# Fewer plain experts in the first token group, and three group change-overs laid out over two periods

## The chip, the cores and the metric

The kernel runs on one core of a Trainium2 chip. The metric is the device time of one execution in microseconds (us), as a median of several runs. The core's engines are TensorE (PE; its weight loads are listed apart as PEld), VectorE (DVE), ScalarE (ACT), GpSimd (POOL) and SyncE (SP), which here only issues DMAs. Each engine works off its own list of instructions in order.

## The reference, cut to what matters

A banded attention is followed by a first layer with an ELU between two matrix products, and by eight experts without routing: each token's row goes through every expert, and the results are added with weights P.

```python
x = attention(q, k, v)                      # 2304 tokens, 512 wide
h = x @ w_in                                # 512 -> 2048
x = elu(h) @ w_out                          # 2048 -> 512
P = exp(x @ w_gate - max)                   # 2304 x 8, then 8 rounds of
...                                         # row and column normalising
out = 0
for e in range(8):
    out += P[:, e:e + 1] * (maximum(x @ w1[e], 0) @ w2[e])   # 512 -> 1024 -> 512
```

## The kernel before, in words

All products are made at nearly full float32 precision: each operand is split into a high part (what the matmul keeps of it) and a low part (the rest), and three matmuls are added: high by high, high by low and low by high.

**The first layer** is cut into four hidden quarters ("layer pairs", `u` from 0 to 3). The last ends where the first expert matmul starts, at 554.8 us; it has 20 steps, each one hidden block of 128 for one block of up to 512 tokens. `step_in` makes the hidden values, `elu` turns them over on ACT and DVE, and `step_out` multiplies them out two steps later.

**The experts** take the 2304 tokens in three groups of 768. The first group (tokens 0 to 767, in blocks of 512 and 256) is computed **plainly** for all eight experts: `e_in` (lines 740 to 742) multiplies x by w1, `relu` splits the result, `e_out` (lines 758 to 760) multiplies by w2, and `e_done` (line 778) adds the weighted result to the accumulator `acc` on DVE. The steps are walked in units; from the second expert on a unit is half an expert (four hidden blocks of 128 for both token blocks, eight steps). I call that a **half**.

Groups 1 and 2 are computed **by a Strassen scheme**: the quarters of x, w1 and w2 are combined into seven forms each, so that seven products take the place of eight. A **period** `(g, e, pp)` is half an expert for one group: seven steps `j`, in each of which `l1` (line 914) makes two of the 14 products with the x forms `xf`, and `l2` (line 988) one of the seven products with the w2 forms, eight steps later (`LAG`). In `l1` PE adds up several products in one PSUM bank (`la`), and ACT copies the intermediate sums out (`keep`, line 927, tiles `a`, `u`, `v`) before PE may go on in that bank. DVE adds (`c`, lines 922 and 944; `s`, line 931), ACT and DVE split into high and low (`h`), POOL makes the low parts of the sums (line 896). DVE adds `l2`'s results into `acc2` (lines 1007 and 1009).

**The weight forms** are made once, while the first group runs, and do both jobs: a plain unit uses them in SBUF (the pure quarters, in one of eight slots `f0` to `f7`), and all seven are stored to DRAM (`wdi`, `wdo`) for the periods. There are 64 of them, `h = (expert * 4 + p) * 2 + m`. One form is five tasks (`p_tasks`): two pairs of sums on POOL (`p_sums`, line 645), two high parts on ACT (`p_high`, line 670), two low parts on DVE (`p_low`, line 675), two stores (`p_store`, lines 680 and 681) and the loads for the form after next but one (`p_load`, lines 631 and 636). The order of the work is written out by hand: at the end of each step the main loop runs as many tasks as a clock allows (`goal = 5 * (4 + clock / 3)`; a half is 12 clock units, so four forms a half). All DMAs go through SP's one queue.

**A change of group** needs new x forms. `x_load` fetches x from DRAM (`x2d`), `x_sums` and `x_t4` make four sums on DVE (line 833, 768 wide), and `x_form` makes each of the seven forms by a copy on ACT (line 828) and a subtraction on POOL (line 829). `x_steps` puts all of it in the last period of the old group: loads at step 0, the first form and three sums at step 2, the rest at steps 4 to 6. The first set of x forms is made in the last plain unit by the same functions. `oa` is the group's accumulator `acc2`; it has one buffer, so the first use by a new group waits for the stores of the old one's output (line 1012).

Of the kernel before, what the change touches and what calls it, by code (L numbers as in the profile page):

```python
# [8 lines left out]
F32 = mybir.dt.float32  # L9
# [9 lines left out]
def kernel(  # L19
# [14 lines left out]
    nc = tc.nc  # L34
# [578 lines left out]
    ]  # L613
    NHU = E * NP * 2
    rws, sws, forms = {}, {}, {}
# [4 lines left out]

    def p_load(h):
        if h >= NHU:
            return
        e, p, m = p_at(h)
# [38 lines left out]
    def p_high(h, part):  # L663
        if part == 0:
            b = h % 8
# [11 lines left out]
    def p_store(h):  # L677
# [3 lines left out]
        nc.sync.dma_start(out=to[:, 3:7], in_=r(forms[h][:, 4:8]))  # L681

    def p_tasks(h):
        def begin():
            p_sums(h, 0)

        def sums():
            p_sums(h, 1)  # L690
            if h:
                p_high(h - 1, 1)

        def lows():
            if h:
                p_low(h - 1, 1)

        def highs():
            p_high(h, 0)
            if h:  # L700
                p_store(h - 1)

        def last():
            p_low(h, 0)
            p_load(h + 3)

        def end():
            p_high(h, 1)
            p_low(h, 1)
            p_store(h)  # L710

        return [begin, sums, lows, highs, last] + ([end] if h == NHU - 1 else [])

# [9 lines left out]
    eunits = [(0, (0, 1)), (0, (2, 3)), (0, (4, 5, 6, 7))]  # L723
    eunits += [(e, tuple(range(4 * h, 4 * h + 4))) for e in range(1, E) for h in range(2)]

# [40 lines left out]
    def e_done(u, j, jj, pa):  # L766

        e, ch = eunits[u]
        a = acc[j][:, jj * DM:(jj + 1) * DM]
        tt = j * TB // P + jj  # L770
        if u == 0:
            nc.scalar.activation(a, pa, AF.Copy)  # L772
        elif e == 0:
            nc.vector.tensor_tensor(out=a, in0=pa, in1=a, op=ALU.add)
        else:
            if e == 1 and ch[0] == 0:
                nc.vector.tensor_scalar(a, a, Pr[:, tt, 0:1], None, op0=ALU.mult)
# [5 lines left out]
    x2d = {  # L783
        j: tc.dram_tile([P, NCC, n], F32, name=f"x2d{j}") for j, (t0, n) in enumerate(blocks)
        if t0 + n > 2 * TH
    }

    def x2_store(j):
        if j in x2d:
            nc.sync.dma_start(out=x2d[j], in_=acc[j].rearrange("p (c t) -> p c t", c=NCC))  # L790

# [42 lines left out]

    def x_sums():
        t1 = xs["pool"].tile([P, 2, TH], F32, tag="t1", name="xt1")
        t2 = xs["pool"].tile([P, 2, TH], F32, tag="t2", name="xt2")
        xs["t1"], xs["t2"] = t1, t2
        x_sum(t1, xs[0, 1], xs[0, 0])
        x_sum(t2, xs[1, 1], t1)  # L840
        x_sum(xs[0, 1], xs[1, 1], xs[0, 1])

    def x_t4():
        x_sum(xs[1, 0], xs[1, 0], xs["t2"])
        x_form(6, xs[1, 0])


    x_steps = {
        2: [lambda: x_form(0, xs[0, 0]), x_sums],
        4: [lambda: x_form(1, xs[1, 0]), lambda: x_form(4, xs["t2"])],  # L850
        5: [lambda: x_form(5, xs[0, 1]), lambda: x_form(3, xs["t1"])],
        6: [lambda: x_form(2, xs[1, 1]), x_t4],
    }

# [116 lines left out]
    def l2(k, x):  # L971
        g, e, pp = periods[k]
        pi = out_order[x]
        if x == 0:
            banks.reverse()
            ot["A"] = P2["ps2"].tile([P, 1024], F32, tag=banks[0], bufs=1, name=banks[0])
            if e == 0 and pp == 0:
                oa[g] = P2["ap"].tile([P, 6, DM], F32, tag="acc2", name="acc2")
# [39 lines left out]
    with tc.manual_schedule():  # L1018
# [127 lines left out]
        queue = []  # L1146
        extra = []
        for s, st in enumerate(steps):
            u, j, i = st
# [14 lines left out]
            if u == NU - 1:  # L1164
                if su == 2:
# [4 lines left out]
                    open_pool("A1", "right")  # L1170
                    for h in range(3):
                        p_load(h)
                    ptasks += p_tasks(0) + p_tasks(1) + p_tasks(2)[:3]
                elif su > 8 and ptasks:
                    ptasks.pop(0)()
            if extra:
# [5 lines left out]
        ]  # L1182
        ptasks += [f for h in range(2, NHU) for f in p_tasks(h)][3:]

        clock = 0
        ntask = 13
        done2 = False
        xq = []
        for s, st in enumerate(esteps):
# [24 lines left out]
            goal = 5.0 * (4.0 + clock / 3.0)  # L1214
            if s >= 2:
                lim = 5 * (NHU if done2 else 4) + 3
                while ptasks and ntask < min(goal, lim):
                    ptasks.pop(0)()
                    ntask += 1
            if u == len(eunits) - 1:  # L1220
                if (j, x) == (0, 1):
# [8 lines left out]
                    xq += [f for fs in x_steps.values() for f in fs]  # L1230
                for _ in range(2):
                    if xq:
                        xq.pop(0)()
# [12 lines left out]
        for s in range(NPD * 7 + LAG):  # L1246
# [8 lines left out]
            while after and k >= NPD:  # L1255
                after.pop(0)()
            if s == 1:
                for n in range(NW2):
                    w2_load(n)
            if s >= LAG:  # L1260
                l2(*divmod(s - LAG, 7))
                w2_load(s - LAG + NW2)
            if k + 1 < NPD and periods[k + 1][0] != periods[k][0]:
                if j == 0:
                    x_load(periods[k + 1][0])
                for f in x_steps.get(j, []):
                    f()
                if j == 6:
                    close(xs["cm"])
        close(ps2_cm)  # L1270
# [37 lines left out]
```

## Time and profile before

| what | us |
|---|---|
| three runs: median (lowest to highest) | 2081.74 (2080.84 to 2083.01) |
| the profiled execution: its own time | 2082.14 |
| its span, first to last instruction | 2080.1 |
| PE busy / DVE / ACT / POOL | 2042.9 / 1387.5 / 797.7 / 691.8 |
| the plain experts, first e_in to first l1 | 554.8 to 1109.7 |
| the 32 Strassen periods, first l1 to the end | 1109.7 to 2080.1 |

The profiled execution is 0.4 us above the median, and 2.0 us of its time lie outside its span. PE is busy nearly all the time, so a count of PE's busy time says little of where time could be saved; what counts is how long PE takes for a stage of known size, and where it is held up. The stretches are therefore compared by time for the same number of matmuls.

### The profile page before, as it was taken

How to read it: one execution, taken by the hardware profiler on the slowest of the kernel's cores; microseconds unless marked ns; L12 is line 12 of the kernel's file. 1: busy time of each engine (PE TensorE's matmuls, PEld its weight loads, DVE VectorE, ACT ScalarE, POOL GpSimd, SP SyncE). 2: the span in 40 equal slices, each digit the busy share in tenths (PEclk: the TensorE clock that was granted, in tenths of full speed). 3: DMA queues.
4: the chain of work that ended last, by engine and by line, in shares of the span. 5: the costliest groups of instructions: out<-in, count | busy, mean ns of one | idle time of the engine just before them, and what ended most of it. 6: DMA issues, size and time to landing. Idle time of an engine off the chain costs nothing.

```text
span 2080.1 us, 35944 instructions
## 1 busy us (share of the span) xinstructions
PE 2042.9 (98%) x13336; PEld 1866.0 (90%) x13336; DVE 1387.5 (67%) x2687; ACT 797.7 (38%) x1680; POOL 691.8 (33%) x698
## 2 busy tenths in 40 slices
PE   8999999999999999999999999999998999999998
PEld 6788888888878888888888999999998999999998
DVE  7944876754586555555555777777777777777776
ACT  5676333334442333333333333333334333333332
POOL 5533221220053434343333333233335323332332
PEclk9999999999999999999999999999999999999999
DMA  7631111110296878787777878787886887877874
GB/s 167 133 87 25 51 53 40 51 31 21 112 349 247 302 271 300 269 294 273 290 273 263 252 248 248 252 250 246 252 269 216 273 246 251 250 247 250 252 247 132
DMA packets 265469, 430.76 MB, mean 207 GB/s; under 512 B 75536, under 2 KB 139088, under 8 KB 260816
## 3 DMA queue, kind: packets, MB, share of 16 engines
q1 hardware_dynamic: 265216, 428.44, 63.4%
q8 instruction: 106, 1.74, 0.3%
q14 instruction: 67, 0.55, 0.1%
q10 hardware_dynamic: 80, 0.03, 0.0%
HBM read 302.53 MB, written 125.83 MB: 206 GB/s over the span
## 4 chain that ended last, share of the span: by engine, by line
PE 84%; DVE 6%; issue 6%; DMA 1%; POOL 1%; ACT 1%; SPq 0%; DVEq 0%; POOLq 0%; ACTq 0%
PE la L914 13%; PE ob L988 11%; PE oa L988 11%; PE lb L914 9%; PE ac L760 4%; PE ac L759 4%; PE ac L758 4%; PE p L740 4%; PE p L741 4%; PE p L742 4%; PE p L189 3%; PE p L191 2%; PE p L190 2%; PE ac L491 2%; PE ac L490 2%
## 5 line engine op out<-in xcount | busy, mean ns | idle before, releaser
L896 POOL TENSOR_TENSOR h<-s,h 128x384 fp32r<-128x384 f32 x256 | 314.2, 1246 | 620.7 <-ACT h L887 564.9
L914 PE MATMUL la<-xf,w1f 128*128 128x384 f32 x1536 | 307.7, 338 | 9.4 <-ACT u L927 5.1
L914 PEld LDWEIGHTS la<-xf,w1f 128*128 128x128 f32 x1536 | 264.8, 190 | 11.4 <-ACT u L927 6.0
L645 POOL TENSOR_TENSOR sw<-rw 128x256 f32<-128x256 f32 x128 | 123.7, 967 | 407.1 <-issue 203.9
L988 PE MATMUL oa<-w2f,h 128*128 128x256 f32 x2016 | 258.0, 282 | 1.1 <-DVE acc L1009 1.1
L988 PE MATMUL ob<-w2f,h 128*128 128x256 f32 x2016 | 258.7, 282 | 0.0
L988 PEld LDWEIGHTS oa<-w2f,h 128*128 128x128 f32 x2016 | 253.7, 190 | 1.4 <-DVE acc L1009 1.4
L988 PEld LDWEIGHTS ob<-w2f,h 128*128 128x128 f32 x2016 | 254.6, 190 | 0.0
L892 DVE SCALAR_TENSOR_TENSOR h<-c,h 128x384 fp32r<-128x384 f32 x192 | 176.2, 918 | 102.6 <-ACT h L887 102.0
L914 PE MATMUL lb<-xf,w1f 128*128 128x384 f32 x1152 | 232.8, 336 | 0.1
L232 DVE SCALAR_TENSOR_TENSOR hl<-p,hh 128x256 fp32r<-128x256 f32 (+1 forms) x128 | 71.1, 556 | 201.3 <-ACT hh L231 201.2
L914 PEld LDWEIGHTS lb<-xf,w1f 128*128 128x128 f32 x1152 | 201.1, 189 | 0.5 <-DVE c L944 0.4
L231 ACT ACTIVATE hh<-p 128x256 fp32r<-128x256 f32 (+1 forms) x128 | 62.8, 490 | 336.1 <-PE p L742 331.2
L887 ACT ACTIVATE h<-s 128x384 fp32r<-128x384 f32 x256 | 130.2, 523 | 121.4 <-DVE s L931 49.9
L740 PE MATMUL p<-xh,f 128*128 128x256 f32 (+1 forms) x512 | 174.0, 340 | 0.0
L741 PE MATMUL p<-xl,f 128*128 128x256 f32 (+1 forms) x512 | 173.0, 338 | 0.0
L742 PE MATMUL p<-xh,f 128*128 128x256 f32 (+1 forms) x512 | 172.5, 337 | 0.0
L1009 DVE SCALAR_TENSOR_TENSOR acc<-oa,Pr,acc 128x256 f32<-128x256 f32 x330 | 138.7, 474 | 37.8 <-PE oa L988 37.8
L887 ACT ACTIVATE h<-c 128x384 fp32r<-128x384 f32 x192 | 100.5, 523 | 148.0 <-DVE c L922 104.9
L1009 DVE SCALAR_TENSOR_TENSOR acc<-ob,Pr,acc 128x256 f32<-128x256 f32 x318 | 133.6, 474 | 34.6 <-PE ob L988 34.6
L758 PE MATMUL ac<-f,hh 128*128 128x512 f32 x384 | 151.9, 396 | 2.2 <-ACT acc L772 2.2
L760 PE MATMUL ac<-f,hl 128*128 128x512 f32 x384 | 151.7, 395 | 0.3 <-DVE hl L232 0.3
(147 smaller groups left out, 3954.0 us busy)
## 6 DMA issues: line engine op xcount, KB each, us to landing
w1f<-wdi SPq DMA_DIRECT2D x448, 256.0 KB, 3.8
w2f<-wdo SPq DMA_DIRECT2D x224, 512.0 KB, 4.0
rw<-in_moe_w_dram SPq DMA_DIRECT2D x256, 128.0 KB, 2.8
wdi<-f SPq DMA_DIRECT2D x32, 1024.0 KB, 6.0
wdo<-f SPq DMA_DIRECT2D x32, 1024.0 KB, 5.5
wdi<-f SPq DMA_DIRECT2D x32, 768.0 KB, 4.1
wdo<-f SPq DMA_DIRECT2D x32, 768.0 KB, 4.3
raw<-in_moe_w_in_dram SPq DMA_DIRECT2D x16, 512.0 KB, 3.9
```

What stands on the lines that cost most here:

```text
L645: nc.gpsimd.tensor_tensor(out=sw[:, o], in0=a, in1=b, op=op)
L740: nc.tensor.matmul(p1[:, :n], w[:, s, 0, cs], xh, start=(c == 0), stop=False)
L741: nc.tensor.matmul(p1[:, :n], w[:, s, 0, cs], xl, start=False, stop=False)
L742: nc.tensor.matmul(p1[:, :n], w[:, s, 1, cs], xh, start=False, stop=(c == NCC - 1))
L758: nc.tensor.matmul(o, gh[:, tcs], wh, start=(x == 0), stop=False)
L760: nc.tensor.matmul(o, gl[:, tcs], wh, start=False, stop=l)
L887: nc.scalar.activation(h[:, 0], src, AF.Relu if relu else AF.Copy)
L892: nc.vector.scalar_tensor_tensor(h[:, 1], src, 0.0, r(h[:, 0]), op0=ALU.max, op1=ALU.subtract)
L896: nc.gpsimd.tensor_tensor(out=h[:, 1], in0=src, in1=r(h[:, 0]), op=ALU.subtract)
L914: nc.tensor.matmul(o, w[:, a, c, :], x[:, b, c, :], start=first and c == 0 and z == 0, stop=last and c == 1 and z == 2, skip_group_check=True,
L988: nc.tensor.matmul(o[:, c * HB2:(c + 1) * HB2], hs[p][:, a, c * P:(c + 1) * P], w[:, p, b, :], start=fresh and c != 1 and p == 0 and z == ...
L1009: nc.vector.scalar_tensor_tensor(a, src, pe, a, op0=ALU.mult, op1=ALU.add)
```

## The change

Experts 6 and 7 of the first group leave the plain part: they become four more periods `(0, 6, 0)` to `(0, 7, 1)` ahead of the others, so that there are 36 periods and six plain experts. The result of the six plain experts goes to DRAM (`accd`) and is read back as the first group's `acc2`. The list `order` sets in which order forms are made: the eight of expert 7 first, beside the last layer pair of the first layer (in two slots), with two of expert 0; then four to a half as before, and in eight halves a fifth, one of expert 6. The x of all three groups is stored to `x2d`. The x forms of a new group are made by a plan of single pieces over the last two periods of the old group and the first two steps of the new one, with sums 384 wide.

```diff
-    NHU = E * NP * 2
+    KP = 6
+    order = [((E - 1) * 2 * NP + i, i % 2) for i in range(2 * NP)]
+    NPRE = len(order) + 2
+    for u in range(2 * KP):
+        hs = [(4 * u + i, (4 * u + i) % 8) for i in range(4)]
+        if 0 <= u - 2 < (E - 1 - KP) * 2 * NP:
+            hs.insert(1, (KP * 2 * NP + u - 2, hs[3][1]))
+        order += hs
...
-    eunits += [(e, tuple(range(4 * h, 4 * h + 4))) for e in range(1, E) for h in range(2)]
+    eunits += [(e, tuple(range(4 * h, 4 * h + 4))) for e in range(1, KP) for h in range(2)]
...
         if u == len(eunits) - 1:
-            nc.sync.dma_start(out=out[tt * P:(tt + 1) * P, :], in_=a)
+            nc.sync.dma_start(out=accd[:, tt], in_=a)
...
-    periods = [(g, e, pp) for g in range(1, NG2) for e in range(E) for pp in range(NP // 2)]
+    periods = [
+        (g, e, pp)
+        for g in range(NG2) for e in range(0 if g else KP, E) for pp in range(NP // 2)
+    ]
...
+    def x_part(n, c):
...
+        o, a, b = (
+            ("t1", (0, 1), (0, 0)), ("t2", (1, 1), "t1"), ((0, 1), (1, 1), (0, 1)),
+            ((0, 0), (1, 0), "t2"),
+        )[n]
+        x_sum(xs[o][:, c], xs[a][:, c], xs[b][:, c])
+
+    def x_plan(slot):
+        if slot in (1, 3, 4, 5, 6, 7):
+            i = (1, 3, 4, 5, 6, 7).index(slot)
+            x_part(i // 2, i % 2)
+        elif slot in (10, 12):
+            x_part(3, (slot - 10) // 2)
+        for s, f, nm in (
+            (9, 0, (0, 0)), (11, 1, (1, 0)), (11, 4, "t2"), (12, 5, (0, 1)), (13, 3, "t1"),
+            (14, 2, (1, 1)), (15, 6, (0, 0)),
+        ):
+            if s == slot:
+                x_form(f, xs[nm])
...
-                elif su > 8 and ptasks:
-                    ptasks.pop(0)()
+                elif su > 2:
+                    while ntask < min(5 * NPRE + 3, 3.4 * (su - 2)):
+                        ptasks.pop(0)()
+                        ntask += 1
...
+        due = [0.0] * (5 * (NPRE + 2))
+        for u in range(1, 2 * KP):
+            n = 5 if 0 <= u - 2 < (E - 1 - KP) * 2 * NP else 4
+            due += [12.0 * (u - 1 + (i + 1) / (5 * n)) for i in range(5 * n)]
...
-                while ptasks and ntask < min(goal, lim):
+                while ptasks and ntask < lim and due[ntask] <= clock:
...
-                    x_load(1)
+                    x_load(0)
...
             if s == 1:
+                oa[0] = P2["ap"].tile([P, 6, DM], F32, tag="acc2", bufs=1, name="acc2")
+                nc.sync.dma_start(out=oa[0], in_=accd)
                 for n in range(NW2):
                     w2_load(n)
...
-            if k + 1 < NPD and periods[k + 1][0] != periods[k][0]:
-                if j == 0:
-                    x_load(periods[k + 1][0])
-                for f in x_steps.get(j, []):
-                    f()
-                if j == 6:
-                    close(xs["cm"])
+            for k2 in (k, k + 1, k + 2):
+                if k >= 0 and 0 < k2 < NPD and periods[k2][0] != periods[k2 - 1][0]:
+                    slot = 7 * (k - k2 + 2) + j
+                    if slot == 0:
+                        x_load(periods[k2][0])
+                    x_plan(slot)
+                    if slot == 16:
+                        close(xs["cm"])
```

Three places show how instructions move. The first is DVE at a change of group, before: step 2 of the last period of group 1 (`xt` and `xb` are the loaded pieces of x and their sums, `c` and `s` are l1's sums, `acc` is l2's accumulation).

```order
L944 TENSOR_TENSOR c_16411<-lb,v 128x384
L892 SCALAR_TENSOR_TENSOR h_16413<-c_16411,h_16413 128x384
L1009 SCALAR_TENSOR_TENSOR acc_11214<-oa,Pr,acc_11214 128x256 x3
L833 TENSOR_TENSOR xt_16456<-xb_16352,xb_16350 128x768
L833 TENSOR_TENSOR xt_16457<-xb_16357,xt_16456 128x768
L833 TENSOR_TENSOR xb_16352<-xb_16357,xb_16352 128x768
L931 SCALAR_TENSOR_TENSOR s_16469<-c_16411,r_16467 128x384
L931 SCALAR_TENSOR_TENSOR s_16473<-c_16317,s_16469 128x384
```

With the change the same sums stand at steps 3, 4 and 5 of the last period but one:

```order
L1031 SCALAR_TENSOR_TENSOR acc_11864<-oa,Pr,acc_11864 128x256 x3
L849 TENSOR_TENSOR xt_16685<-xb_16634,xb_16632 128x384
L944 TENSOR_TENSOR c_16809<-lb,a 128x384
L914 SCALAR_TENSOR_TENSOR h_16811<-c_16809,h_16811 128x384
L1031 SCALAR_TENSOR_TENSOR acc_11864<-ob,Pr,acc_11864 128x256 x3
L849 TENSOR_TENSOR xt_16686<-xb_16639,xt_16685 128x384
L966 TENSOR_TENSOR c_16870<-lb,v 128x384
L914 SCALAR_TENSOR_TENSOR h_16872<-c_16870,h_16872 128x384
L1031 SCALAR_TENSOR_TENSOR acc_11864<-oa,Pr,acc_11864 128x256 x3
L849 TENSOR_TENSOR xt_16686<-xb_16639,xt_16685 128x384
```

Three sums of 768 stood in a row between two steps; now one of 384 stands between two steps.

The second place is SP where the plain part hands over to the periods (`w1f`, `w2f` are weight forms for the periods), before and with the change:

```order
L865 DMA w1f<-wdi_1_105 128x512 x4
L780 DMA out_dram<-acc_97 128x512 x4
L780 DMA out_dram<-acc_98 128x512 x2
L865 DMA w1f<-wdi_1_105 128x512 x2
L865 DMA w1f<-wdi_2_106 128x512 x2
L876 DMA w2f<-wdo_0_136 128x1024 x7
```

```order
L887 DMA w1f<-wdi_1_129 128x512 x4
L796 DMA accd<-acc_97 128x512 x4
L796 DMA accd<-acc_98 128x512 x2
L887 DMA w1f<-wdi_1_129 128x512 x2
L887 DMA w1f<-wdi_2_130 128x512 x2
L1287 DMA acc_10122<-accd 128x3072
L898 DMA w2f<-wdo_0_148 128x1024 x7
```

The six stores of the plain result go to `accd` in the place of the output, and one load of 1.57 MB that must wait for them stands ahead of the w2 forms.

The third place is SP beside the last layer pair (`rw` is a raw weight, `wdi_0_132` a form of expert 7), from the first loads on, before and with the change:

```order
L631 DMA rw<-in_moe_w_dram 128x2x128 x4
L790 DMA x2d_152<-acc_98 128x2048
L636 DMA rw<-in_moe_w_dram 128x256 x4
L680 DMA wdi_0_104<-f_5767 128x1536
L681 DMA wdi_0_104<-f_5767 128x2048
```

```order
L647 DMA rw<-in_moe_w_dram 128x256 x4
L691 DMA wdi_0_132<-f_5423 128x1536
L692 DMA wdi_0_132<-f_5423 128x2048
L642 DMA rw<-in_moe_w_dram 128x2x128 x4
L691 DMA wdo_0_150<-f_5508 128x3x512
L692 DMA wdo_0_150<-f_5508 128x4x512
L647 DMA rw<-in_moe_w_dram 128x256 x4
L803 DMA x2d_152<-acc_97 128x2048
```

Two forms are stored ahead of the first store of x, where none was.

## Rows read from the trace of the kernel before

**Rows 1.** The page: granted clock in 40 slices, and the chain that ended last.

```profile
PEclk9999999999999999999999999999999999999999
PE 84%; DVE 6%; issue 6%; DMA 1%; POOL 1%; ACT 1%; SPq 0%; DVEq 0%; POOLq 0%; ACTq 0%
```

**Rows 2.** Busy time by stretch: twelve plain halves, ten Strassen periods (columns: first row).

```profile
core 0: us, PE busy (x) PEld busy (x) DVE busy (x) ACT busy (x) POOL busy (x), PEclk, DMA share, GB/s
672.80:1073.10 400.30, 400.30 (x2017) 338.35 (x2016) 220.09 (x267) 138.23 (x192) 160.38 (x192) 1.00 0.78 284
1217.40:1513.20 295.80, 295.80 (x2102) 295.80 (x2101) 215.31 (x411) 106.64 (x221) 98.08 (x81) 1.00 0.80 249
```

**Rows 3.** Groups by line and shape, 672.8 to 1073.1 us: xcount | busy, mean ns | idle.

```profile
L758 PE MATMUL ac<-f,hh 128*128 128x512 f32 x288 | 113.3, 393 | 0.0
```

**Rows 4.** The same view, 1217.4 to 1513.2 us.

```profile
L914 PE MATMUL la<-xf,w1f 128*128 128x384 f32 x480 | 94.9, 335 | 0.0
```

**Rows 5.** Line 914 by stretch: the four periods round the group change.

```profile
1513.20:1542.80 29.60, 15.75 (x84) 14.34 (x85) 1.00 0.82 250
1542.80:1576.20 33.40, 16.87 (x85) 14.97 (x86) 0.95 0.80 269
1576.20:1611.30 35.10, 17.39 (x85) 15.86 (x86) 0.95 0.68 209
1611.30:1642.20 30.90, 16.27 (x84) 14.19 (x85) 1.00 0.87 289
```

**Rows 6.** Timeline of that change: start, us, instruction [idle before <-releaser].

```profile
1556.90 1.18 DVE L833 TENSOR_TENSOR xt<-xb,xb 128x768 f32<-128x768 f32 x1
1567.10 1.15 PE L914 MATMUL la<-xf,w1f 128*128 128x384 f32 x3 [1.92 <-ACT u L927]
1580.58 2.35 DVE L833 TENSOR_TENSOR xb<-xb,xt 128x768 f32<-128x768 f32 x1
1584.24 1.22 PE L914 MATMUL la<-xf,w1f 128*128 128x384 f32 x3 [3.70 <-ACT a L927]
1623.49 1.27 DVE L1007 TENSOR_SCALAR acc<-ob,Pr 128x256 f32<-128x256 f32 x3 [4.87 <-DMA out_dram<-acc]
```

**Rows 7.** Timeline of an undisturbed period: steps 3 to 5.

```profile
1601.58 0.54 DVE L922 TENSOR_TENSOR c<-lb,a 128x384 f32<-128x384 f32 x1
1602.99 0.47 ACT L927 ACTIVATE u<-la 128x384 f32<-128x384 f32 x1
1603.87 1.20 PE L914 MATMUL la<-xf,w1f 128*128 128x384 f32 x6
```

**Rows 8.** The view of rows 3: a form's work in twelve halves.

```profile
L645 POOL TENSOR_TENSOR sw<-rw 128x256 f32<-128x256 f32 x96 | 93.0, 969 | 236.2 <-issue 177.9 <-DVE f L675 33.5 <-DMA rw<-in_moe_w_dram 24.7
L675 DVE TENSOR_TENSOR f<-sw,f 128x1024 fp32r<-128x1024 f32 x49 | 64.6, 1318 | 2.5 <-ACT f L670 2.5
L670 ACT ACTIVATE f<-rw 128x1024 fp32r<-128x1024 f32 x48 | 50.5, 1053 | 0.0
```

**Rows 9.** The page's DMA issues: KB each, median us from issue to landing.

```profile
wdi<-f SPq DMA_DIRECT2D x32, 1024.0 KB, 6.0
wdi<-f SPq DMA_DIRECT2D x32, 768.0 KB, 4.1
xb<-x2d SPq DMA_DIRECT2D x4, 384.0 KB, 5.4
```

**Rows 10.** The view of rows 2: stretches with much DMA traffic.

```profile
590.00:610.00 20.00, 19.29 (x84) 15.04 (x85) 16.69 (x34) 8.15 (x13) 7.26 (x11) 0.91 1.01 386
672.80:706.00 33.20, 33.20 (x169) 28.27 (x168) 18.55 (x25) 11.51 (x16) 14.18 (x16) 1.00 0.86 305
1125.00:1130.00 5.00, 4.36 (x14) 3.85 (x13) 1.45 (x3) 1.51 (x3) 0.00 (x0) 0.50 1.04 408
```

**Rows 11.** The same view: inside the last layer pair.

```profile
500.00:520.00 20.00, 20.00 (x91) 16.27 (x90) 8.92 (x15) 9.26 (x15) 0.00 (x0) 1.00 0.13 54
```

**Rows 12.** Line 914 by stretch, as rows 5: the first period.

```profile
1109.70:1130.60 20.90, 17.79 (x84) 16.85 (x84) 0.84 0.92 329
```

More of the change, by code (lines that the diff above doesn't have):

```diff
@@ L613 @@
     ]
-    NHU = E * NP * 2
+    KP = 6
[6 more added lines that the diff above has]
+        order += hs
+    assert sorted(h for h, _ in order) == list(range(E * NP * 2))
     rws, sws, forms = {}, {}, {}
@@ L619, in p_at, with p_load @@
         return h // (2 * NP), h // 2 % NP, h % 2
-    def p_load(h):
-        if h >= NHU:
+    def p_load(n):
+        if n >= len(order):
             return
+        h = order[n][0]
         e, p, m = p_at(h)
@@ L664, in p_high @@
         if part == 0:
-            b = h % 8
+            b = slot_of[h]
             forms[h] = pools["A1" if b < 2 else "A2" if b < 4 else "B"].tile(
@@ L681, in p_store, with p_tasks @@
         nc.sync.dma_start(out=to[:, 3:7], in_=r(forms[h][:, 4:8]))
-    def p_tasks(h):
+    slot_of = dict(order)
+    def p_tasks(n):
+        h = order[n][0]
+        before = order[n - 1][0] if n else None
         def begin():
@@ L690, in sums @@
             p_sums(h, 1)
-            if h:
-                p_high(h - 1, 1)
+            if n:
+                p_high(before, 1)
         def lows():
-            if h:
-                p_low(h - 1, 1)
+            if n:
+                p_low(before, 1)
         def highs():
             p_high(h, 0)
-            if h:
-                p_store(h - 1)
+            if n:
+                p_store(before)
         def last():
             p_low(h, 0)
-            p_load(h + 3)
+            p_load(n + 3)
         def end():
@@ L710, in end @@
             p_store(h)
-        return [begin, sums, lows, highs, last] + ([end] if h == NHU - 1 else [])
+        return [begin, sums, lows, highs, last] + ([end] if n == len(order) - 1 else [])
     ptasks = []
@@ L779, in e_done @@
         if u == len(eunits) - 1:
-            nc.sync.dma_start(out=out[tt * P:(tt + 1) * P, :], in_=a)
[L783 to L786, printed above, removed]
+            nc.sync.dma_start(out=accd[:, tt], in_=a)
+    x2d = [tc.dram_tile([P, NCC, n], F32, name=f"x2d{j}") for j, (_, n) in enumerate(blocks)]
+    accd = tc.dram_tile([P, 6, DM], F32, name="accd")
     def x2_store(j):
-        if j in x2d:
-            nc.sync.dma_start(out=x2d[j], in_=acc[j].rearrange("p (c t) -> p c t", c=NCC))
+        nc.sync.dma_start(out=x2d[j], in_=acc[j].rearrange("p (c t) -> p c t", c=NCC))
     P2 = {}
@@ L833, in x_sum @@
         nc.vector.tensor_tensor(out=o, in0=a, in1=b, op=op)
[L835 to L853, printed above, removed]
+    def x_part(n, c):
+        if (n, c) == (0, 0):
+            for nm in ("t1", "t2"):
+                xs[nm] = xs["pool"].tile([P, 2, TH], F32, tag=nm, name=f"x{nm}")
+        o, a, b = (
[15 more added lines that the diff above has]
+                x_form(f, xs[nm])
     w1t, w2t = {}, {}
@@ L976, in l2 @@
             ot["A"] = P2["ps2"].tile([P, 1024], F32, tag=banks[0], bufs=1, name=banks[0])
-            if e == 0 and pp == 0:
+            if k and periods[k - 1][0] != g:
                 oa[g] = P2["ap"].tile([P, 6, DM], F32, tag="acc2", name="acc2")
@@ L1147 @@
         extra = []
+        ntask = 0
         for s, st in enumerate(steps):
@@ L1170 @@
                     open_pool("A1", "right")
-                    for h in range(3):
-                        p_load(h)
-                    ptasks += p_tasks(0) + p_tasks(1) + p_tasks(2)[:3]
-                elif su > 8 and ptasks:
-                    ptasks.pop(0)()
+                    for n in range(3):
+                        p_load(n)
+                    ptasks += [f for n in range(len(order)) for f in p_tasks(n)]
+                elif su > 2:
+                    while ntask < min(5 * NPRE + 3, 3.4 * (su - 2)):
+                        ptasks.pop(0)()
+                        ntask += 1
             if extra:
@@ L1182 @@
         ]
-        ptasks += [f for h in range(2, NHU) for f in p_tasks(h)][3:]
         clock = 0
-        ntask = 13
+        due = [0.0] * (5 * (NPRE + 2))
+        for u in range(1, 2 * KP):
+            n = 5 if 0 <= u - 2 < (E - 1 - KP) * 2 * NP else 4
+            due += [12.0 * (u - 1 + (i + 1) / (5 * n)) for i in range(5 * n)]
+        due += [due[-1]]
+        assert len(due) == 5 * len(order) + 1
         done2 = False
@@ L1213 @@
             clock += nb[j] // 256
-            goal = 5.0 * (4.0 + clock / 3.0)
             if s >= 2:
-                lim = 5 * (NHU if done2 else 4) + 3
-                while ptasks and ntask < min(goal, lim):
+                lim = len(due) if done2 else 5 * (NPRE + 2) + 3
+                while ptasks and ntask < lim and due[ntask] <= clock:
                     ptasks.pop(0)()
@@ L1226 @@
                     P2["w1p_cm"], P2["w1p"] = pool("w1p", side="right")
-                    x_load(1)
+                    x_load(0)
                     for n in range(NW1):
                         w1_load(n)
-                    xq += [f for fs in x_steps.values() for f in fs]
-                for _ in range(2):
+                    xq += [lambda s=s: x_plan(s) for s in range(1, 16)]
+                for _ in range(3):
                     if xq:
```

## The prediction, made before the changed kernel ran

> **What bounds the kernel now.** I read the chain of waits first. PE holds 84% of it, and the granted clock is full in all 40 slices of the page [rows 1]; so the question for each stage is how long PE takes for it, and where PE is held up. Next I read two long undisturbed stretches by window: PE is busy for the whole of both, DVE for 55% of the plain one and 73% of the Strassen one, ACT and POOL for less than 41% [rows 2]. There PE sets the pace. Then I compared equal pieces of work, counted by matmuls, for what a plain expert and a Strassen expert cost. Then I looked for the places where PE does not keep that pace: the change of group [rows 5, 6] and the hand-over from the plain part to the periods [rows 12]. "The sum" below is made against the profiled execution's 2082.1 us, 0.4 us above the median of 2081.74.
>
> **1. Two experts change from plain to Strassen.** A half has 24 matmuls of line 758 (4 hidden blocks, 6 token tiles). 288 of them in 400.3 us [rows 2, 3] are 12 halves: 33.36 us each, 66.72 us an expert. A period has 48 matmuls into `la` (8 of its 14 products, 6 each). 480 of them in 295.8 us [rows 2, 4] are ten periods: 29.58 us each, 59.16 us an expert. Two experts give 2 x (66.72 - 59.16) = **15.1 us**. Both rates are PE's own, so nothing hides this gain. It is lost only if another resource can't follow in one of the two parts, which points 3 to 5 go through.
>
> **2. The changes of group.** Before there is one, after there are two. The four periods round the present one take 29.6, 33.4, 35.1 and 30.9 us [rows 5]; against 29.58 that is 10.7 us too much (3.8, 5.5 and 1.3). The timeline names three causes. First, the three sums at step 2 keep DVE for 3 us (1.2, then two of 0.95; the first of them is shown), DVE's `c` comes late, ACT stands at its `h` copy, and its copy `u` behind that holds PE for 1.92 us at 1567.10. Second, the fourth sum at 1580.58 takes 2.35 us, ACT waits for it in order with a form, its copy `a` is behind that form, and PE stands for 3.70 us [rows 6]. After each the granted clock falls: 0.95 over both periods [rows 5], which at half speed (1.2 instead of 2.4 GHz) is 5% x 2 of each, so 3.3 and 3.5 us at half pace and about 1.7 us lost in each. Third, `acc2` has one buffer, DVE waits 4.87 us for the output's stores [rows 6], and that period is 1.3 us long [rows 5].
>
> The change takes the first two causes apart: each piece of DVE work between two steps is one sum of 384, and the fourth sum stands at steps 3 and 5 of the last period, while the form that needs it follows only at step 1 of the new one, three steps (over 12 us) later. The third cause stays as it is. What comes new: a sum at step 3 stands ahead of the add `c<-lb,a`. In an undisturbed period that add starts at 1601.58, ACT's `u` ends at 1603.46 and PE starts on that bank at 1603.87 [rows 7], so there is 0.4 us of room. A sum of 384 costs half of one of 768: 0.6 us by 1.18, 1.2 us by 2.35 [rows 6]. So PE is held for 0.2 to 0.8 us, twice in each change (steps 3 of both periods). The first sum also comes one step after the loads, and the pieces land 5.4 us after issue [rows 9]; a step is 29.58 / 7 = 4.2 us, so DVE may stand for a microsecond or two, in a step with few DVE instructions. The bounds for one change of group are 1.3 us (the stores alone) and 5.3 us (half of today's). I take 1.3 + 2 x 0.5 = 2.3 and round up to 2.4, since none of the stalls is then long enough to be followed by a clock drop as those of 1.92 and 3.70 us were. Together: -10.7 + 2 x 2.4 = **-5.9 us**.
>
> **3. Five forms in a half in place of four, in eight halves.** Per form POOL has 0.97 + 0.97 + two shorter sums, under 3.9 us; ACT two copies of 1.05; DVE two subtractions of 1.32 or less [rows 8]. A fifth form per 33.36 us takes POOL from 13.4 to 17, ACT from 11.5 to 13.6, DVE from 18.3 to 21 us: all with room. DMA is the tight one. Its share over twelve halves is 0.78 [rows 2], and 48 forms were made there (96 sums of line 645, two a form [rows 8]): 0.78 x 400.3 / 48 = 6.50 us of all 16 engines for one form. Five forms need 32.5 of 33.36 us, a share of **0.975**; in bytes 284 x 1.25 = 355 GB/s. If the queue can be kept filled it fits, and the loads are issued ahead, two forms (10 tasks of 33.36 / 25 us, 13 us) before POOL needs them, which bridges a backlog. That such a rate is reached is shown by 20 us at 386 GB/s with a share of 1.01, and 408 GB/s for 5 us [rows 10]. If it does not fit, the loads come late, ACT stands at a form's copy, and the copy `hh` of a plain step behind it holds PE. Bounds: nothing, or the rival below; I take **+0.5 us**.
>
> Here a page weighs in. The Trainium skill, in "DMA: Bandwidth & Descriptors", section "Where 436 GB/s comes from", says that traffic between HBM and SBUF is bound by HBM at about 358 GB/s for a core. By it five forms fit into a half with 1% to spare, and any pause of the queue would be lost for good; the 386 and 408 GB/s of this trace stand above that figure, so the measurement decides, and the page only makes me give the rival below more than I else would.
>
> **4. Expert 7's forms beside the last layer pair.** 53 tasks (10.6 forms) run there in place of 13. In that stretch PE is busy throughout, DVE for 45%, ACT for 46%, POOL not at all, and DMA stands at 0.13 [rows 11]. Eight more forms add 8 x 2.6 = 21 us to DVE and 17 us to ACT over some 90 us, 0.24 and 0.19 of the time: both stay below 0.7. With two slots, a slot's store must land before the second form after it is begun, five tasks or about 1.5 steps later; 768 and 1024 KB land 4 to 6 us after issue [rows 9], so ACT can stand for 1 or 2 us at every second form. The ELU's result is used two steps later, which hides that. If the cover fails it is 4 x 2 us. I take **+0.5 us**. The one more store of x (1 MB) falls into an idle queue.
>
> **5. The hand-over.** The first period takes 20.9 us with DMA at 0.92 [rows 12], and at 1125 to 1130 us the share is 1.04 [rows 10]. The load of `acc2` (128 x 3072 x 4 bytes, 1.57 MB) stands in SP's queue ahead of the w2 forms and the next w1 forms, and waits for the last store. At 408 GB/s it is 3.9 us of DMA. PE's stop there is due to ACT's copies, not to a transfer, so the load can cost nothing, or up to 3.9 us if w1 forms now come late. 12 of them are loaded ahead; I take **+0.5 us**.
>
> **The sum:** -15.1 - 5.9 + 0.5 + 0.5 + 0.5 = -19.5; 2082.1 - 19.5 = 2062.6, and against the median, 0.4 lower, **2062.2 us**. If each change of group cost only the 1.3 us of the stores and the other terms nothing, it would be 2082.1 - 15.1 - 10.7 + 2.6 = 2059; with stalls hidden besides, 2056. With 5.3 for each and the 3.9 of the hand-over, 2082.1 - 15.1 + 3.9 = 2071. So the likeliest case's own range is 2056 to 2071.
>
> **Rivals.**
>
> (a) *The changes of group stay as dear as today.* The first sum would wait for the loads with DVE's queue behind it, or the forms' subtractions on POOL would come late for the new period. Two at 10.7 give 2082.1 - 15.1 + 10.7 = 2077.7; from 5.3 each on, 2071. For it speaks that x is loaded only one step ahead of its first use, and the 0.4 us of room in [rows 7]; against it that both of today's long stalls come from a row of DVE work which is now spread. Chance 0.12.
>
> (b) *DMA cannot follow the five forms* (the slower side). If the queue keeps only a share s busy, a half takes 32.5 / s. At 0.97 or more nothing is lost; at 0.90 it is 36.1 us, 8 x 2.7 = 22 us, the whole gain, about 2084; at 0.86, the most that any of the halves had that I looked at [rows 10], it is 37.8 us, 8 x 4.4 = 35 us, about 2098. It decides from s = 0.91 down. For it: four forms leave gaps in the queue now, and SP waits in order for stores and loads. Against it: those gaps are there because nothing more is due, and 1.01 held for 20 us. Chance 0.10: a third of it still faster, a fifth the same.
>
> (c) *The hand-over or the last layer pair costs its upper bound*, 3.9 or 8 us: 2066 to 2070. Chance 0.06.
>
> **How the numbers follow.** My forecast has 0.72. What a measurement can tell is about 0.2%, 4.2 us, so faster means under 2077.6. Faster: 0.72 + 0.06 + 0.08 of (a) + 0.03 of (b) = 0.89. The same: 0.03 of (a) and 0.02 of (b), 0.05. Slower: 0.05 of (b) and 0.01 for changes of group dearer than today. The range is 2056 to 2077: it leaves out half of (a), most of (b) and a little below, together under 0.2.
>
> **What would show it.** The plain halves with five forms still 33.4 us, DMA share there near 0.97 and PE without waits on `hh`; 36 periods, 32 or so of them at 29.6 us; in the periods round both changes of group no PE stall over 1.5 us, the granted clock at 1.00, and DVE's wait for the output's stores in both; a first period near 21 us. The forecast is wrong if plain halves lengthen to 34 us or more, or a change of group costs over 5 us.

## The result and the profile after

| | before | after |
|---|---|---|
| median of the runs, us (lowest to highest) | 2081.39 (2080.84 to 2083.01) | 2064.64 (2063.17 to 2065.59) |
| span of the profiled execution, us | 2080.1 | 2062.5 |
| ratio, 95% interval | | 0.9919 [0.9903, 0.9934] |

The forecast was 2062.2 us, the range 2056 to 2077. The kernel became faster by 16.8 us (17.6 by the two spans); 19.5 were forecast. So the direction and most of the size were right, and the rest of this text asks where the missing 2 to 3 us went and whether the terms were right one by one, or only their sum.

The page first, the lines that answer to [rows 1]:

```profile
PEclk9999999999999999999999999999999999999999
PE 88%; DVE 7%; DMA 3%; ACT 1%; issue 1%; SPq 0%; DVEq 0%; ACTq 0%
```

PE still holds most of the chain that ended last. Next the plain part: busy time by stretch over nine halves (behind the five engines stand the granted clock, the DMA share and GB/s), over the first seven of them, which make five forms each (the last two make four), in three single halves with five forms, and the group by which the nine are counted.

```profile
644.70:945.20 300.50, 300.50 (x1516) 253.79 (x1515) 182.63 (x223) 116.99 (x158) 153.54 (x172) 1.00 0.93 338
644.70:878.50 233.80, 233.80 (x1180) 197.43 (x1179) 144.87 (x179) 93.94 (x126) 126.88 (x140) 1.00 0.97 353
711.50:745.00 33.50, 33.50 (x169) 28.12 (x168) 19.93 (x25) 13.44 (x19) 18.04 (x20) 1.00 1.02 365
745.00:778.20 33.20, 33.20 (x169) 28.27 (x168) 20.00 (x25) 13.41 (x19) 18.03 (x20) 1.00 0.97 358
811.70:844.90 33.20, 33.20 (x169) 28.28 (x168) 20.00 (x25) 13.42 (x19) 18.03 (x20) 1.00 0.95 350
```
```profile
L774 PE MATMUL ac<-f,hh 128*128 128x512 f32 x216 | 85.0, 393 | 0.0
```

216 matmuls are nine halves of 24: 300.5 / 9 = 33.39 us each, as before [rows 2, 3]. PE is busy for all of it, although the DMA share went from 0.78 to 0.97 over the halves with five forms. The Trainium skill ("DMA: Bandwidth & Descriptors", "Where 436 GB/s comes from") gives about 358 GB/s as the bound for a core's traffic between HBM and SBUF. This trace does not agree: one half moved 365 GB/s, the seven together 353, and PE set the pace in all of them. The experiment with six forms, below, shows what the ceiling is.

Then the changes of group: line 936, `l1`, by stretch, answering to [rows 5]. The first four rows stand round the first change, the last three round the second.

```profile
1030.00:1061.20 31.20, 16.16 (x85) 14.32 (x86) 1.00 0.85 287
1061.20:1091.00 29.80, 15.95 (x85) 14.25 (x86) 1.00 0.78 246
1091.00:1120.60 29.60, 15.76 (x85) 14.34 (x86) 1.00 0.79 248
1120.60:1150.60 30.00, 16.03 (x84) 14.25 (x85) 1.00 0.89 298
1505.70:1535.80 30.10, 16.02 (x85) 14.26 (x86) 1.00 0.86 293
1535.80:1565.60 29.80, 15.98 (x84) 14.23 (x85) 1.00 0.80 253
1595.20:1625.00 29.80, 15.92 (x85) 14.34 (x86) 1.00 0.90 301
```

The excess over 29.58 is 1.6 + 0.2 + 0.4 = 2.2 us at the first and 0.5 + 0.2 + 0.2 = 0.9 us at the second, where 10.7 stood before; the granted clock stays at 1.00. The timeline has the one stall of note, and the wait for the output's stores:

```profile
1042.66 0.56 DVE L849 TENSOR_TENSOR xt<-xb,xb 128x384 f32<-128x384 f32 x1 [2.70 <-DMA xb<-x2d]
1053.64 1.31 PE L936 MATMUL la<-xf,w1f 128*128 128x384 f32 x6 [1.17 <-ACT u L949]
1131.88 1.27 DVE L1029 TENSOR_SCALAR acc<-ob,Pr 128x256 f32<-128x256 f32 x3 [3.95 <-DMA out_dram<-acc]
```

DVE waits for the loaded x one step after the loads, and 11 us later PE stands for 1.17 us. The last place is the last layer pair of the first layer. Its 20 steps hold 80 matmuls of line 189 for each product, which counts them; the first row is of before, the second of after.

```profile
445.05:554.80 109.75, 29.82 (x80) 14.95 (x80) 1.00 0.16 56
```
```profile
446.45:560.30 113.85, 29.82 (x80) 14.97 (x80) 0.99 0.65 231
```

It became 4.1 us longer. No PE wait stands in the pair before, and one after. The timeline at its end, first the gate's copy `lgT` and the small gate matmuls before, then after:

```profile
553.11 0.67 DVE L522 COPY lgT<-lg 16x512 f32<-16x512 f32 x1
553.86 1.05 PE L531 MATMUL lt<-sel,lgT 16*128 16x8 f32 x8
```
```profile
556.73 1.23 DVE L686 TENSOR_TENSOR f<-sw,f 128x1024 fp32r<-128x1024 f32 x1 [0.52 <-ACT f L681]
557.88 0.67 DVE L522 COPY lgT<-lg 16x512 f32<-16x512 f32 x1
558.60 1.77 PE L531 MATMUL lt<-sel,lgT 16*128 16x8 f32 x8 [3.00 <-DVE lgT L522]
```

PE now stands for 3.00 us until DVE has copied the gate logits out, and DVE comes to it only after a form's low part. Stretches of 15 us show DVE ahead of that, first before the change, then after, and what follows:

```profile
540.00:555.00 15.00, 15.00 (x98) 13.54 (x98) 10.49 (x19) 6.38 (x15) 2.87 (x4) 1.00 0.37 148
```
```profile
540.00:555.00 15.00, 15.00 (x96) 13.39 (x95) 13.16 (x17) 7.94 (x16) 7.44 (x8) 1.00 0.74 271
555.00:570.00 15.00, 12.00 (x52) 10.06 (x51) 6.65 (x12) 5.15 (x10) 2.99 (x4) 0.77 0.78 298
```

DVE was busy for 13.16 of 15 us where it had been for 10.49, and then the granted clock is 0.77 on average: 0.23 x 2 x 15 = 6.9 us at 1.2 instead of 2.4 GHz. The pair ends at 560.3 us, so much of that half clock falls into the first expert. This expert takes as long as before, first row before, second after, but not for the same reasons; the third row is a stall of before.

```profile
554.80:639.20 84.40, 78.47 (x398) 64.87 (x398) 65.47 (x133) 33.07 (x50) 32.62 (x36) 0.96 0.76 278
```
```profile
560.30:644.70 84.40, 79.62 (x397) 65.88 (x397) 65.47 (x133) 34.88 (x52) 34.31 (x38) 0.95 0.83 305
```
```profile
590.71 0.50 PE L758 MATMUL ac<-f,hh 128*128 128x512 f32 x1 [2.21 <-ACT acc L772]
```

Its first step is 2.4 us longer after (6.7 against 4.3), at half clock. The step in which before had the stall of 2.21 us is 3.6 us shorter (4.6 against 8.2), since that stall is gone. It is still there with the plan alone (2.22 us at 592.1 us) and in no kernel with the new order of the forms, so it went with that order; how is not shown. The three steps at its end are 1.6 us longer. So the late copy cost about 4.1 + 2.4 = 6.5 us, and a gain that nobody had forecast hid a part of it.

### The profile page after: what moved, and what is told of

Read it like the earlier page. It is cut to its first block, busy times and chain, and to the rows that moved or that the text cites. A ratio compares the mean times of both kernels' runs of the same rounds, so it can differ in the third digit from the quotient of the medians.

```text
span 2062.5 us, 36791 instructions
## 1 busy us (share of the span) xinstructions
PE 2029.4 (98%) x13504; PEld 1872.6 (91%) x13504; DVE 1440.0 (70%) x2811; ACT 829.3 (40%) x1743; POOL 757.1 (37%) x737
## 4 chain that ended last, share of the span: by engine, by line
PE 88%; DVE 7%; DMA 3%; ACT 1%; issue 1%; SPq 0%; DVEq 0%; ACTq 0%
PE la L936 14%; PE ob L1010 12%; PE oa L1010 12%; PE lb L936 10%; PE p L189 3%; PE p L756 3%; PE p L757 3%; PE p L758 3%; PE ac L774 3%; PE ac L775 3%; PE ac L776 3%; PE p L191 3%; PE p L190 3%; PE ac L491 2%; PE ac L489 2%; PE ac L490 2%
## 5 line engine op out<-in xcount | busy, mean ns | idle before, releaser
L918 POOL TENSOR_TENSOR h<-s,h 128x384 fp32r<-128x384 f32 x288 | 353.7, 1247 | 671.0 <-ACT h L909 601.9
L936 PE MATMUL la<-xf,w1f 128*128 128x384 f32 x1728 | 344.3, 337 | 4.8 <-ACT u L949 4.0
L1010 PE MATMUL oa<-w2f,h 128*128 128x256 f32 x2268 | 290.2, 282 | 0.8 <-DVE acc L1031 0.8
L1010 PEld LDWEIGHTS oa<-w2f,h 128*128 128x128 f32 x2268 | 285.4, 190 | 1.0 <-DVE acc L1031 1.0
L231 ACT ACTIVATE hh<-p 128x512 fp32r<-128x512 f32 (+1 forms) x96 | 47.2, 492 | 246.7 <-PE p L758 246.5
L232 DVE SCALAR_TENSOR_TENSOR hl<-p,hh 128x512 fp32r<-128x512 f32 (+1 forms) x96 | 53.4, 557 | 127.7 <-ACT hh L231 127.7
L189 PE MATMUL p<-xh,w0h 128*128 128x512 f32 (+1 forms) x384 | 132.1, 344 | 0.0
L756 PE MATMUL p<-xh,f 128*128 128x256 f32 (+1 forms) x384 | 131.8, 343 | 0.0
L757 PE MATMUL p<-xl,f 128*128 128x256 f32 (+1 forms) x384 | 130.8, 341 | 0.0
L758 PE MATMUL p<-xh,f 128*128 128x256 f32 (+1 forms) x384 | 130.4, 340 | 0.0
L191 PE MATMUL p<-xh,w0l 128*128 128x512 f32 (+1 forms) x384 | 129.3, 337 | 0.0
```

The source lines that it names most:

```text
L189: nc.tensor.matmul(p1, w1h[:, c, :], xh[:, c, :], start=(c == 0), stop=False)
L191: nc.tensor.matmul(p1, w1l[:, c, :], xh[:, c, :], start=False, stop=(c == NCC - 1))
L756: nc.tensor.matmul(p1[:, :n], w[:, s, 0, cs], xh, start=(c == 0), stop=False)
L757: nc.tensor.matmul(p1[:, :n], w[:, s, 0, cs], xl, start=False, stop=False)
L758: nc.tensor.matmul(p1[:, :n], w[:, s, 1, cs], xh, start=False, stop=(c == NCC - 1))
L918: nc.gpsimd.tensor_tensor(out=h[:, 1], in0=src, in1=r(h[:, 0]), op=ALU.subtract)
```

## The experiments

The kernel before ran between 2079.99 and 2084.26 us beside these runs, so a median can tell some 2 us apart; smaller effects are read from the stretch where the edit works.

**The group changes put back.** The Strassen part of the changed kernel with the old placement.

```diff
-            for k2 in (k, k + 1, k + 2):
-                if k >= 0 and 0 < k2 < NPD and periods[k2][0] != periods[k2 - 1][0]:
...
+            if 0 <= k and k + 1 < NPD and periods[k + 1][0] != periods[k][0]:
+                if j == 0:
+                    x_load(periods[k + 1][0])
+                for f in x_steps.get(j, []):
+                    f()
```

> The changed kernel with the old placement of the group changes in the Strassen part: loads at step 0 and all sums and forms at steps 2 to 6 of the last period. Theory (the row of DVE sums was what cost 10.7 us a change): the periods round each of the two changes cost 9 to 11 us in excess again instead of 2.2 and 0.9, time 2080 to 2084, about that of the kernel before. Rival (the change of group got cheap for another reason, such as other traffic): time stays at 2065 to 2068.

Measured: 2081.48 us, ratio to the kernel before 0.9997 [0.9988, 1.0007]. Line 957 (`l1`) by stretch, two periods at each change, and the two PE stalls of the first:

```profile
1059.10:1092.40 33.30, 16.82 (x85) 14.89 (x86) 0.95 0.81 274
1092.40:1127.50 35.10, 17.39 (x84) 15.84 (x85) 0.95 0.67 208
1542.60:1575.90 33.30, 16.04 (x85) 14.38 (x85) 0.95 0.80 271
1575.90:1611.00 35.10, 16.62 (x85) 14.89 (x86) 0.95 0.67 209
```
```profile
1083.33 2.11 PE L957 MATMUL la<-xf,w1f 128*128 128x384 f32 x6 [1.91 <-ACT u L970]
1100.47 2.17 PE L957 MATMUL la<-xf,w1f 128*128 128x384 f32 x6 [3.70 <-ACT a L970]
```

The stalls of 1.9 and 3.7 us and the clock of 0.95 are back, at both changes, each to a tenth of a microsecond as in [rows 5, 6]. Without the new plan the exchange of two experts gains nothing: a third group needs a second change, and an old-style change costs about 9.2 us in these two periods.

**The plan alone.** The kernel before (eight plain experts, one change of group) with the changed kernel's `x_part`, `x_plan` and the loops that call them, for the first set of x forms too.

```diff
-                    xq += [f for fs in x_steps.values() for f in fs]
+                    xq += [lambda s=s: x_plan(s) for s in range(1, 16)]
-                for _ in range(2):
+                for _ in range(3):
...
-            if k + 1 < NPD and periods[k + 1][0] != periods[k][0]:
+            for k2 in (k, k + 1, k + 2):
+                if k >= 0 and 0 < k2 < NPD and periods[k2][0] != periods[k2 - 1][0]:
...
```

> The kernel before with only the new plan for the x forms: eight plain experts, one change of group. Theory (the two parts add up): the one change of group goes from 10.7 to 1 to 2 us in excess, time 2071 to 2073, so that the exchange of two experts is worth 6 to 8 us of the whole 16.7. Rival (the plan only pays because there are two changes, or the new plan is no cheaper by itself): 2078 or more.

Measured: 2073.05 us (2071.31 to 2074.76), 0.9958 [0.9942, 0.9975], at the upper edge of what was expected. The two periods with the plan and the one with the wait of the accumulator:

```profile
1512.50:1543.40 30.90, 16.06 (x85) 14.31 (x86) 1.00 0.87 291
1543.40:1573.20 29.80, 15.95 (x84) 14.24 (x85) 1.00 0.78 246
1602.80:1632.40 29.60, 15.77 (x85) 14.34 (x86) 1.00 0.91 305
```

The change of group is down to 1.5 us. So of the 16.8 us about 9 are the plan's on the old work (2082.05 beside this run, less 2073.05), and about 8 come from the exchange with all that it brings: 15.1 less one more change of group, the longer layer pair and a start of the pair that is 1.4 us later.

**Six forms in a half.** Three experts leave the plain part; the forms of two of them are made in the eight halves.

```diff
-    KP = 6
+    KP = 5
...
-        if 0 <= u - 2 < (E - 1 - KP) * 2 * NP:
+        if 0 <= u - 2 < 2 * NP:
             hs.insert(1, (KP * 2 * NP + u - 2, hs[3][1]))
+            hs.insert(2, ((KP + 1) * 2 * NP + u - 2, hs[3][1]))
```

> Three experts leave the plain part instead of two: expert 5's forms are made with expert 6's, so that eight halves make six forms each. Theory (a form needs 6.5 us of the 16 DMA engines, and at five forms they are at 0.97): six need 39 us, more than the 33.36 us of PE's work, so those halves lengthen to 37 to 39 us, POOL and ACT wait for raw weights or free slots and PE waits for ACT; time 2064.6 - 7.5 + 8 x (3.6 to 5.6) = 2086 to 2102. Rival (DMA is not the bound at this rate, because its share counts overlapped packets): halves stay at 33.4 us and time falls to about 2057.

Measured: 2088.9 us (2086.14 to 2094.96, three runs), 1.0038 [1.002, 1.0057]. Four halves by stretch, and waits of 680 to 940 us (us in total, times, longest), PE's own last:

```profile
682.00:832.00 150.00, 142.79 (x685) 117.68 (x683) 101.05 (x107) 61.91 (x81) 105.66 (x99) 0.97 1.04 382
```
```profile
DVE f L687 <- ACT f L682: 58.9, 23, 7.8
ACT f L682 <- POOL sw L657: 43.7, 25, 3.3
POOL sw L657 <- DMA rw<-in_moe_w_dram: 35.6, 17, 6.7
ACT f L682 <- DMA wdi<-f: 31.4, 3, 10.9
PE ac L775 <- ACT hh L231: 8.6, 6, 1.8
```

The first two plain halves still take 33.6 and 33.2 us; in this stretch a half takes 150 / 4 = 37.5 us. The DMA share is 1.04 (packets overlap a little), 382 GB/s, and the chain is the one that point 3 of the prediction named: raw weights come late, then POOL, then ACT, whose `hh` holds PE. ACT also waits for a slot's store to land, which was not named there. The ceiling is 37.5 / 6 = 6.25 us a form, so five forms fill 31.3 of 33.36 us, 94%. The 358 GB/s of the Trainium skill ("DMA: Bandwidth & Descriptors", "Where 436 GB/s comes from") is exceeded for 150 us, so for this mix of loads and stores on one core the measured 382 decides. By an estimate with 358 as the bound, six forms would have taken 40 us a half.

**The layer pair, two cures.** First the copy of the gate logits by another engine, then the form tasks at a higher rate, so that they end before the last gate work.

```diff
-        nc.vector.tensor_copy(t[:, :n], lg[:2 * E, :n])
+        nc.scalar.activation(t[:, :n], lg[:2 * E, :n], AF.Copy)
```

> The copy of the gate logits out of PSUM goes from DVE to ACT; nothing else changes. Theory (DVE is crowded beside the last layer pair, its copy of the logits comes late, PE stands for 3.00 us before the small gate matmuls and then runs 6.8 us at half clock): the stall and the clock drop behind it go, the last layer pair takes about 110 us again instead of 113.8, time about 2060 (2058 to 2061.5). Rival (ACT or the queue of PE itself is late there, as forms in two slots hold ACT): the stall stays near 3 us, time 2064 to 2066.

Measured: 2063.98 us (2062.24 to 2064.92), not to be told from 2064.64, and above what was expected. The stall is half gone:

```profile
555.60 1.04 ACT L681 ACTIVATE f<-sw 128x1024 fp32r<-128x1024 f32 x1
556.55 0.57 ACT L522 ACTIVATE lgT<-lg 16x512 f32<-16x512 f32 x1
557.17 1.05 PE L531 MATMUL lt<-sel,lgT 16*128 16x8 f32 x8 [1.62 <-ACT lgT L522]
```

The pair takes 111.8 us (446.4 to 558.2). On ACT, too, the copy stands behind a form's instruction, so it seems that what matters is not the engine but that form work stands ahead of the copy. The second cure tests that:

```diff
-                    while ntask < min(5 * NPRE + 3, 3.4 * (su - 2)):
+                    while ntask < min(5 * NPRE + 3, 4.0 * (su - 2)):
```

> The 53 form tasks beside the last layer pair run at 4.0 a step instead of 3.4, so they end two steps before the pair does. Theory (DVE is crowded by form work that falls among the gate work of the last blocks): the PE stall of 3.00 us before the gate matmuls shrinks below 1.5 us and no clock drop follows it, time 2060 to 2062. Rival (the total of form work in the pair is what costs, wherever it falls, since a slot must be stored before it is used again): stalls of ACT and PE appear earlier in the pair and the pair stays at about 114 us, time 2064 to 2066.

Measured: 2059.97 us (2059.28 to 2060.78), 0.9892 [0.9878, 0.9907]. The pair by line 189, two stretches inside it, and the gate matmuls:

```profile
445.30:555.10 109.80, 29.82 (x80) 14.98 (x80) 1.00 0.74 267
```
```profile
500.00:520.00 20.00, 20.00 (x91) 16.14 (x90) 16.36 (x19) 11.91 (x18) 8.89 (x10) 1.00 0.99 357
540.00:555.00 15.00, 15.00 (x99) 13.51 (x97) 10.53 (x19) 6.67 (x16) 2.88 (x4) 1.00 0.89 336
```
```profile
551.39 0.68 DVE L522 COPY lgT<-lg 16x512 f32<-16x512 f32 x1
554.15 1.05 PE L531 MATMUL lt<-sel,lgT 16*128 16x8 f32 x8
```

The pair is back at 109.8 us with the same form work, DMA at 0.99 for 20 us, DVE at 0.82 in mid-pair, and PE never waiting. So it is the place of the work, not its amount: the rival falls. The first expert's first step takes 4.3 us again. In this execution the period at the second change in which DVE waits for the accumulator is a long one:

```profile
1589.70:1621.40 31.70, 16.33 (x85) 14.26 (x86) 1.00 0.86 284
```

**The first sum one step later.**

```diff
-        if slot in (1, 3, 4, 5, 6, 7):
-            i = (1, 3, 4, 5, 6, 7).index(slot)
+        if slot in (2, 3, 4, 5, 6, 7):
+            i = (2, 3, 4, 5, 6, 7).index(slot)
```

> The first DVE sum of a group change stands two steps behind the loads instead of one. Theory (at one step behind, DVE waits 2.70 us for the loaded x, its next add is late, and PE stands for 1.17 us three steps later): DVE's wait and that PE stall go, the period that took 31.1 us takes about 29.9, time about 1.3 us less, 2063.3. Rival (the stall is due to the sum at step 3 standing ahead of an add): the period stays at 31 us, time unchanged at 2064.6.

Measured: 2063.64 us (2061.97 to 2064.05), which the medians do not settle. In the trace the period in question does, with the first sum below it:

```profile
1028.60:1058.40 29.80, 16.01 (x84) 14.30 (x84) 1.00 0.89 293
```
```profile
1042.91 0.55 DVE L849 TENSOR_TENSOR xt<-xb,xb 128x384 f32<-128x384 f32 x1
```

DVE no longer waits, and 31.2 us have become 29.8. The sum at step 3 stays where it was, so it was not that. The other traces agree: at the first change this period takes 29.8 us in all four kernels with the later sum, and 30.5 to 31.5 us in the five other executions that have the first sum one step behind the loads.

**Combinations.** With the gate copy on ACT and the later sum:

> Both edits together: gate logits copied by ACT, first sum two steps behind the loads. If the two causes are independent the gains add up: about 2058.5 (2057 to 2061). If the stalls are only shifted, time stays above 2062.

Measured: 2061.26 us (2060.64 to 2063.12), between the two outcomes that were expected. Its trace has both effects (PE stands for 1.60 us before the gate matmuls, the period takes 29.8 us), but with the half-cure of the pair it does not reach 2058.5. Whether they add up in the time is not shown: each alone moved the median by 1 us or less. Then the changed kernel once more beside the rate of 4.0 with the later sum:

> The changed kernel itself, for a comparison with the next two on one chip: 2064.6 within 1.5 us, the stall before the gate matmuls near 3 us and the period at the first change of group at 31 us again.

Measured: 2063.20 us (2061.78 to 2063.78), with a stall of 2.98 us before the gate matmuls and a period of 31.4 us, as before.

> Form tasks at 4.0 a step beside the last layer pair, and the first sum of a group change two steps behind the loads. Theory (two separate causes, 4.0 us in the pair and about 1.5 us at the changes of group): pair at 110 us, no period round a change over 30.0 us except for the wait of the accumulator, time 2064.6 - 5 = 2059.5, within 1.5 us. Rival (the gain at 4.0 a step alone, 2060.0, was already all there is): no lower than 2060.5.

Measured: 2059.26 us (2057.12 to 2060.40), 0.9890 [0.9873, 0.9906]; about 4 us better than the changed kernel beside it. The medians do not tell this from the rate of 4.0 alone (2059.97); that the later sum helps here too is read from the trace, where the period takes 29.8 us and not 31.5. Last, two buffers for the accumulator:

```diff
-    NW1, NW2, LAG = 12, 7, 8
+    NW1, NW2, LAG = 10, 7, 8
...
-                oa[g] = P2["ap"].tile([P, 6, DM], F32, tag="acc2", name="acc2")
+                oa[g] = P2["ap"].tile([P, 6, DM], F32, tag="acc2", bufs=2, name="acc2")
```

> As the one before, with two buffers for the group accumulator, paid for by ten w1 buffers instead of twelve. Theory (DVE's wait for the output's stores, 4 to 5 us, is what is left of a change of group): the period with that wait goes from 0.2 to 2 us in excess to under 0.1 in both changes, time 0.5 to 2 us lower, about 2058.5. Rival (with two w1 buffers less, PE waits for weights): other periods exceed 29.6 us and time rises by 2 us or more.

Measured: 2059.12 us (2057.64 to 2060.18), the same as the one before. The trace shows both sides; first the two periods in which DVE used to wait for the stores, then a new PE wait in the first period:

```profile
1116.30:1145.90 29.60, 15.76 (x85) 14.34 (x86) 1.00 0.89 300
1590.20:1619.80 29.60, 15.77 (x85) 14.34 (x86) 1.00 0.90 302
```
```profile
997.91 1.98 PE L936 MATMUL la<-xf,w1f 128*128 128x384 f32 x6 [2.70 <-DMA w1f<-wdi]
```

The wait of the accumulator is gone from both (30.5 and 30.3 us in the kernel without the second buffer), and ten weight buffers are too few at the hand-over: the first period takes 23.8 us in place of 20.2. One was paid with the other. The kernel with the rate of 4.0 and the later sum beats both kernels of this study and is as fast as this one.

## Why the prediction was right, point by point

1. *The exchange of two experts, -15.1 us.* Right: the plain halves (33.39) and the undisturbed periods (29.6) kept their lengths, and four periods stand for four halves.
2. *The changes of group, -10.7 + 2 x 2.4.* The mechanism was right (shown by putting the old placement back), the size a little too cautious: 2.2 and 0.9 us, so -7.6 instead of -5.9. Of its pieces, the wait for the accumulator's stores was set at 1.3 us each; PE lost 0.4 and 0.2 us by it here. This piece was in part luck: it differs between executions, and in that of the kernel with the rate of 4.0 the period with this wait at the second change took 31.7 us (its row stands there), 2.1 too much. The sums at step 3 were priced at 0.5 us each; with the first sum out of the way the two periods are 0.2 us too long each. (The room of 0.4 us was read in [rows 7], which lie in the second of the two long periods of [rows 5] and not in an undisturbed one; an undisturbed period has the same 0.4 us, from 1505.44 to 1505.84.) The late first sum, for which the text allowed DVE "a microsecond or two" and PE nothing, held PE for 1.17 us at the first change.
3. *Five forms in a half, +0.5.* It cost nothing. The share was forecast at 0.975 and is 0.97 over the seven halves. Rival (b) is right about the mechanism and wrong about this kernel: it needs six forms.
4. *The last layer pair, +0.5.* This is the term that was mis-sized: it cost 4.1 us in the pair and 2.4 more by the half clock in the step behind it. The prediction looked for a wait of ACT for a slot and a late ELU, summed the engines' busy shares (all below 0.7), and did not look at who waits for DVE with little slack: the gate's copy, which PE needs soon. The mean share came out as forecast, 75.77 of 113.85 us or 0.67 for DVE, but DVE was at 0.88 from 540 to 555 us, ahead of the gate's copy. The upper bound of 8 us did hold it.
5. *The hand-over, +0.5.* The first two periods take 20.8 and 28.1 us against 20.9 and 27.6, and the last plain half 35.9 against 36.6, so about 0.3 us less in all. That does not show that the load of 1.57 MB is hidden: with the plan alone, which has no such load and the same last half of 35.9, the two periods take 19.8 and 27.8 us, so the load may have cost up to 1.3 us and the plan for the first x forms have given it back.

Sum of what was measured: -15.1 - 7.6 + 4.1 - 0.3 = -18.9. The first expert stands in it with nothing, for its gains and losses cancel. The last layer pair also began 1.4 us later in the profiled execution after than in that before, in a part that the change does not touch, which makes -17.5, against -17.6 between the spans. That later start differs from execution to execution (445.3 us in the run with the rate of 4.0), and its cause stays open.

So the total was right to 2.4 us while the two largest misses among the terms were in opposite directions, -1.7 and +3.6, the others -0.5, -0.8 and the start's +1.4. That the total came this close is in part luck: the stall that went from the first expert, 3.6 us, stood in no term, and it paid for more than half of what the late copy cost beyond its price.

## What to carry to other kernels

Work that is moved under another stage is hidden by that stage's average only if nothing there waits for the same engine without slack: look in the stage for short instructions that PE needs at once, and keep bulk work away from just those steps (here a rate of 4.0 instead of 3.4 tasks a step was worth 4 us in the layer pair). A transition that is paid once can become the main cost of a change that makes it happen twice, so it is worth taking apart first. For a shared resource, time per job by its share (6.5 us a form here) tells how many jobs fit, and running one job more than that shows the ceiling.

## What the hardware showed that had not been expected

PE stalls of 1.9 us were followed by a stretch at half clock (0.95 over 33.3 us is 3.3 us at 1.2 GHz) and cost 3.7 us of their period. One of 1.62 us, in the kernel with the gate copy on ACT, was followed by a clock of 0.50 from 559.0 to 562.4 us, while stalls of 1.17 us (changed kernel) and 0.98 us (plan alone, at 1535.82 us) were not followed by any drop. The length of the stall does not decide it alone: in the kernel with six forms, stalls of 1.14 and 0.59 us within 3 us were followed by a clock of 0.66 from 833 to 838 us, and with the plan alone a stall of 2.57 us at 635.79 us left the clock at 1.00. What decides it stays open.

And the DMA queue carried 382 GB/s for 150 us at a share of 1.04, with loads of 512 and 1024 bytes a row among the stores.
